# A linear-attention, mixing and MLP kernel: three low parts move to VectorE, a copy and a split move inside the last attention chunk

## The chip, the cores and the metric

The kernel runs on one core of one Trainium2 chip. The metric is the device time of one execution in microseconds (us); less is better. All times inside the execution are counted from the start of the profiled span.

## The reference

Three layers run one after the other on arrays of 4 batches by 768 tokens by 384 channels, all in float32:

```python
# 1. attention, 32 heads of 48 channels, a 48x48 state per head, token by token
y[:, :, t] = einsum('bhd,bhde->bhe', q[:, :, t], state)
v_old = einsum('bhde,bhd->bhe', state, kt)               # kt: normalised key
state = state + bt * einsum('bhd,bhe->bhde', kt, vt - v_old)
# 2. mixing
theta = x @ w_theta
zr, zi = x * cos(theta), x * sin(theta)
u = x + einsum('ts,bsd->btd', w_tok_r, zr) + einsum('ts,bsd->btd', w_tok_i, zi)
x = u + maximum(u @ w_ch, 0)
# 3. layer norm and a two-layer MLP with a residual
xn = (x - mean) / sqrt(var + 1e-6) * g_ln
out = x + maximum(xn @ w_ch1, 0) @ w_ch2
```

## The kernel before

The attention goes through 24 chunks of 32 tokens (`for c in range(1, NC)`). In a chunk two halves h of the heads take turns. For each half TensorE makes `RW[h]` from the state (`R`), VectorE subtracts it from v (`Rs0` or `Rs1`, L440), TensorE multiplies by a triangular inverse (`W_mm`, L452), ScalarE copies the result to `bdw` in four pieces (L458), TensorE updates the state `S` (L466) and ScalarE copies it to `bds` (L471), which the next `R` of that half reads. The outputs of a chunk are summed in `Y[c]` (`py`) by `yq_work` (L481, from the state) and `ym_work` (L492, from `bdw`); `ym_work` ends with a ScalarE copy `ys` (L498) and four stores from SyncE's queue (L501). In the loop `ym_work` of a chunk is issued in the next chunk; that of the last one, 23, stands behind the loop.

In the last chunks the program slips in work of the mixing layer, by `late(c, k)`: k = 0 comes behind the subtraction of half 0, k = 1 behind that of half 1, and k = 2 at the end of the chunk. Every engine takes its instructions in the order in which the program issues them, and an instruction that waits for another engine holds up all behind it on its own engine.

Two things are slipped in. First, weights. They arrive as pairs of 32-bit words (`raw`, two buffers, and one more later) and are made into float32 `t` by five passes on VectorE (in the late steps L777, L787, L788, L797, L798), and then into a high part (ScalarE, L813) and a low part t - high (L820), since TensorE's fp32r keeps fewer bits. One `wts.step()` does the last two passes of one piece, the next step makes its high and low part and the first three passes of the piece behind it, and so on. A piece of the token weights is 128x768; the weights `W[s]` of token tile s are two pieces. The `split` of a piece says how many of its two rows of the low part go to GpSimd; the rest goes to VectorE. It was None (all on GpSimd) for the tiles 0 and 1 and 0 for the others. The load of a piece (L717) is issued on SyncE's queue, when its `raw` buffer is free.

Second, z of the first mixing steps. `mx.theta` multiplies on TensorE, `mx.angles` takes the nearest whole turn on ScalarE (`kk`, L906) and the rest on VectorE (`nf`, L907), `mx.sines` and `mx.cosines` fill `zf` on ScalarE (L914, L915, L922), `mx.turn` multiplies `zf` by x on VectorE (L931) and makes the high part `zh` on ScalarE (L932), and `mx.rest` makes the low part `zl` on VectorE (L938). There is one `zf` buffer: `mx.sines` of a step fills the one that `mx.rest` of the step before it reads.

Behind the attention the mixing steps follow (`mx.mix`, 24 of them, L957 on TensorE), with the weights made by `wts.pump()`, and then the MLP.

Of the kernel before, what the change touches and what calls it, by code (L numbers as in the profile page):

```python
# [16 lines left out]
NC = 24  # L17
# [75 lines left out]
def attention(ctx, tc, kq, ktok, vin, betai, maskin, x, psa, late=None):  # L93
# [32 lines left out]
    def load_kq(c, part=slice(0, 2)):  # L126
        if c < NC:
            if c not in KQ:
                KQ[c] = ring(c).tile([128, 2, 4, 4, 32], F32, name="kqt")
            nc.sync.dma_start(out=KQ[c][:, part], in_=kq[c][:, part])  # L130

    def load_kt(c):
        if c < NC:
            KT[c] = ktp.tile([128, 4, 2, D], F32, name="ktt")
            nc.sync.dma_start(out=KT[c], in_=ktok[c])

    def load_v(c):
        if c < NC:
            V[c] = vp.tile([128, 8, D], F32, name="vt")
            nc.sync.dma_start(out=V[c], in_=vin[c])  # L140

    def scale_v(c):
        if c < NC:
            k = c % 4
            nc.gpsimd.tensor_tensor(out=V[c], in0=V[c], in1=bc(NT[c // 4][:, 8 * k:8 * k + 8].unsqueeze(2), [128, 8, D]),
                                    op=ALU.mult)
# [284 lines left out]
    def R(h, c):  # L431
        if c == 0:
            return V[0][:, 4 * h:4 * h + 4, :]
        b = bds[h][c % 2]
        for g in range(2):
            for r in range(4):
                nc.tensor.matmul(RW[h][32 * r:32 * r + 32, 0, 2 * g:2 * g + 2, :], KQ[c][:, 0, 2 * h + g, r, :],
                                 b[:, 4 * g + r, :, :], start=True, stop=True)
        Rs = p2.tile([128, 4, D], F32, name=f"Rs{h}")
        nc.vector.tensor_tensor(out=Rs, in0=V[c][:, 4 * h:4 * h + 4, :], in1=RW[h][:, 0, :, :], op=ALU.subtract)  # L440
        return Rs

    def W(h, c, Rs):
        W_mm(h, c, Rs)
        W_out(h, c)
# [14 lines left out]
    def S(h, c):  # L460
        b = bdw[h][c % NB]
        if c == NC - 1:
            return
        for g in range(2):
            for e in range(2):
                nc.tensor.matmul(S_ps[h][64 * e:64 * e + D, g, :], KT[c][:, 2 * h + g, e, :],  # L466
                                 b[:, 2 * g + e, :, :], start=(c == 0 and g == 0), stop=True, skip_group_check=True)
        n = bds[h][(c + 1) % 2]
        for e in range(2):
            ee = slice(64 * e, 64 * e + D)  # L470
            nc.scalar.copy(out=n[ee, :, e, :], in_=S_ps[h][ee, :, :].rearrange("p g (r d) -> p (g r) d", r=4))  # L471
# [3 lines left out]
    def yq_work(wk, c):  # L475
        def first():
            Y[c] = psy.tile([128, 2, 4, D], F32, name="py")

        def q(r):
            for g in range(4):  # L480
                nc.tensor.matmul(Y[c][32 * g:32 * g + 32, :, r, :], KQ[c][:, 1, g, r, :],  # L481
                                 bds[g // 2][c % 2][:, 4 * (g % 2) + r, :, :], start=(r == 0), stop=False,
                                 skip_group_check=True)

        wk.add(0.0, first)
        for r in range(4 if c else 0):
            wk.add(0.24, lambda r=r: q(r))

    def ym_work(wk, c):
        def m(e):  # L490
            for g in range(4):
                nc.tensor.matmul(Y[c][32 * g:32 * g + 32, e, :, :], MT[c][:, g, e, :],  # L492
                                 bdw[g // 2][c % NB][:, 2 * (g % 2) + e, :, :], start=(c == 0 and e == 0),
                                 stop=(e == 1),                                 skip_group_check=True)

        def ev():
            ys = p2.tile([128, 2 * 4 * D], F32, name="ys")
            nc.scalar.copy(out=ys, in_=Y[c].rearrange("p e r d -> p (e r d)"))  # L498
            o = 32 * (c % 4)
            for g in range(4):  # L500
                nc.sync.dma_start(out=x[c // 4][o:o + 32, g, :], in_=ys[32 * g:32 * g + 32, :])  # L501

        for e in range(2):
            wk.add(0.4, lambda e=e: m(e))
        wk.add(0.0, ev)
# [27 lines left out]
    def norms():  # L533
        for s in sorted(norm):
            if ("tg", s) in done:
                norm.pop(s)()
        while pend:
            pend.pop(0)()
# [11 lines left out]
    pe = Work()  # L550
# [53 lines left out]
    for c in range(1, NC):  # L604
        s = c // 4
        step[0] = c
        load_kq(c + 11)
        load_v(c + 5)
        scale_v(c + 2)
        load_kt(c + 2)  # L610
        wa, wm, wq = Work(), Work(), Work()
        for n in {1: (9, 10), 2: (11, 12)}.get(c, (c + 10,)):
            if n < NC:
                a_work(wa, n)
        ym_work(wm, c - 1)
        yq_work(wq, c)
        R0 = R(0, c)
        budget = 2.3 if c >= 14 else 3.08
        if c % 4 == 1 and c > 1 and s + 1 < NS:
            while ("tg", s + 1) not in done:  # L620
                dv.step()
        dv.run(budget)
        if late:
            late(c, 0)
        wa.run((0.0 if c == 2 else 0.42) * wa.left())
        S(1, c - 1)
        W(0, c, R0)
        norms()
        wm.flush()
        R1 = R(1, c)  # L630
        dv.run(budget)
        if late:
            late(c, 1)
        if (c % 4 == 3 and s + 1 < NS) or c == 18:
            while s + 1 not in PT:
                if not dv.step():
                    norms()
        wa.flush()
        S(0, c)
        W(1, c, R1)  # L640
        norms()
        wq.flush()
        if c == 13:
            soon.close()
        if c == 18:
            mid.close()
        if c == 19:
            early.close()
        if late:
            late(c, 2)  # L650
    ym_work(pe, NC - 1)
    pe.flush()


def attn_inputs(q, k, v, beta):
# [173 lines left out]
class Mixer:  # L829
# [21 lines left out]
    def load_w(self, s, wtok, pool, wts, w=None):  # L851
        if pool:
            w = [pool.tile([128, 4, C], F32R, name=f"w{s}_{i}") for i in range(2)]
        self.W[s] = w
        for q in range(2):
            r = slice(2 * q, 2 * q + 2)
            wts.add(("w", s, q), wtok[s, q], lambda r=r: self.W[s][0][:, r], lambda r=r: self.W[s][1][:, r],
                    split=0 if s > 1 else None)

    def trans(self, i):  # L860

# [263 lines left out]
def build(tc, a):  # L1125
# [8 lines left out]
    with tc.manual_schedule(), outer:  # L1134
# [11 lines left out]
        mx = Mixer(nc, x, psa, ident, uT)  # L1146
        wts = Weights(nc, None, wide)

        def late(c, k):
            if (c, k) == (13, 2):  # L1150
                xp2 = ph1.enter_context(tc.tile_pool(name="x_", bufs=1, **R))
                x.extend(xp2.tile([128, 4, C], F32, name=f"x{t}") for t in (4, 5))
            if (c, k) == (18, 2):
                nc.gpsimd.memset(ones.bitcast(F32), 1.0)
                nc.scalar.copy(out=ones, in_=ones.bitcast(F32))
                wts.st = ph1.enter_context(tc.tile_pool(name="st", bufs=1, **R))
                mx.load_theta(ph1, tc, a["wth"], wts)
                wts.load()
                nc.sync.dma_start(out=ident, in_=a["ident"])
                nc.sync.dma_start(out=g, in_=a["g"])  # L1160
            if (c, k) == (19, 2):
                mx.open(ph1, tc)
                for s in range(3):
                    mx.load_w(s, a["wtok"], mx.cst if s < 2 else None, wts)
                wts.load()
            if c > 19 or (c, k) == (19, 1):
                wts.step()
            if (c, k) == (16, 2):
                nc.scalar.activation(out=warm, in_=warm, func=AF.Sin)
            if (c, k) == (20, 2):  # L1170
                mx.trans(0)
            if (c, k) == (21, 2):
                mx.theta(0)
                mx.angles(0)
                mx.trans(1)
            if (c, k) == (22, 1):
                mx.sines()
            if (c, k) == (22, 2):
                mx.cosines()
            if (c, k) == (22, 2):  # L1180
                mx.turn(0)
                mx.rest(0)
            if (c, k) == (23, 0):
                mx.theta(1)
                mx.angles(1)
            if (c, k) == (23, 1):
                mx.sines()
            if (c, k) == (23, 2):
                mx.cosines()

        with ExitStack() as att:
            attention(att, tc, a["kq"], a["ktok"], a["vin"], a["betai"], a["mask"], x, psa, late)
# [46 lines left out]
        for i in range(n):  # L1239
            b, s = MIX[i]  # L1240
# [107 lines left out]
```

## Time and profile before

| what | value |
|---|---|
| time, median of 3 runs | 786.51 us (785.75 to 788.28) |
| profiled execution: its time, its span | 786.73 us, 784.8 us |
| mean granted TensorE clock | 0.969 of full speed |
| busy in the span: TensorE, VectorE, ScalarE, GpSimd | 709.4, 517.8, 356.9, 213.2 us |
| TensorE idle before the first mixing matmul of step 2 (at 250.38 us) | 1.89 us |

The profiled execution took 1.93 us more than its span, and 0.22 us more than the median of the runs. The busy times are sums over stages with different limits: the attention ends and the mixing starts near 230 us, and the MLP takes from some 440 us to the end.

### The profile page before, as it was taken

Reading aid. Unit: us, or ns where it says so; the run is one execution under the profiler, and the core shown is the slowest. Engines: PE = TensorE matmul, PEld = TensorE weight load, DVE = VectorE, ACT = ScalarE, POOL = GpSimd, SP = SyncE. Lnnn points to the kernel's source line nnn. Section 1 sums busy time; section 2 is a strip of 40 time slices with the busy share of each in tenths; the row PEclk is TensorE's granted clock in tenths of the full one; section 3 lists DMA queues with packets and bytes.
Section 4 is the critical chain, followed back from the end, with each engine's and each line's share of the span. In section 5 each row is a group of like instructions: output and inputs, shape, how many; then the busy total and the mean of one; then the engine's idle time right before and its main releaser. Section 6 shows DMA issues by size and latency. Waiting matters only on the chain.

```text
span 784.8 us, 18939 instructions
## 1 busy us (share of the span) xinstructions
PE 709.4 (90%) x7955; PEld 655.4 (84%) x7956; DVE 517.8 (66%) x875; ACT 356.9 (45%) x785; POOL 213.2 (27%) x234
## 2 busy tenths in 40 slices
PE   4577887777778999999997999999999999999997
PEld 3455555554468999999997999999999999999997
DVE  7987989986877888888876755435353534444342
ACT  2276776786775766654444433131322222131211
POOL 5854755744020001211111433113131221121120
PEclk8699999999989999999999999999999999999999
DMA  8975767234444223532432220000000000000000
GB/s 250 248 225 172 201 189 214 83 86 137 153 152 162 88 75 101 165 118 80 121 101 81 101 81 5 26 1 31 1 31 1 31 1 30 1 9 24 1 31 30
DMA packets 29716, 71.39 MB, mean 91 GB/s; under 512 B 4928, under 2 KB 17472, under 8 KB 29632
## 3 DMA queue, kind: packets, MB, share of 16 engines
q1 hardware_dynamic: 29632, 70.19, 29.0%
q8 instruction: 62, 1.02, 0.6%
q14 instruction: 22, 0.18, 0.1%
HBM read 56.02 MB, written 9.44 MB: 83 GB/s over the span
## 4 chain that ended last, share of the span: by engine, by line
PE 64%; DVE 15%; DMA 6%; ACT 6%; issue 5%; POOL 2%; SPq 1%; ACTq 0%; DVEq 0%; POOLq 0%
PE ph L1071 19%; PE acc L1090 19%; PE y L957 11%; PE pc L1012 5%; PE pth L897 3%; DMA bdk<-kq 3%; DVE prod L369 2%; ACT bdw L458 2%; DMA raw<-wtok 2%; PE py L492 1%; PE S L466 1%; PE pa L174 1%; DVE t L797 1%; PE RW L452 1%; DVE Ti L378 1%
## 5 line engine op out<-in xcount | busy, mean ns | idle before, releaser
L957 PE MATMUL y<-w,zh 128*128 128x384 f32 x576 | 154.8, 342 | 3.4 <-DVE u L966 2.4
L1090 PE MATMUL acc<-hh,f 128*128 128x384 f32 x576 | 147.0, 336 | 0.0
L1076 DVE SCALAR_TENSOR_TENSOR hl<-ph,hh 128x384 fp32r<-128x384 f32 x96 | 52.4, 553 | 114.5 <-ACT hh L1075 114.5
L1075 ACT ACTIVATE hh<-ph 128x384 fp32r<-128x384 f32 x96 | 46.7, 491 | 163.0 <-PE ph L1071 163.0
L1071 PE MATMUL ph<-xh,f 128*128 128x384 f32 x576 | 116.4, 337 | 0.4 <-DVE u L966 0.4
L957 PEld LDWEIGHTS y<-w,zh 128*128 128x128 f32 x576 | 105.8, 190 | 4.2 <-issue 2.7
L1090 PEld LDWEIGHTS acc<-hh,f 128*128 128x128 f32 x576 | 104.5, 188 | 0.0
L1071 PEld LDWEIGHTS ph<-xh,f 128*128 128x128 f32 x576 | 101.9, 188 | 0.7 <-issue 0.7
L957 PE MATMUL y<-w,zl 128*128 128x384 f32 x288 | 97.7, 339 | 2.4 <-DVE zl L938 2.4
L1090 PE MATMUL acc<-hl,f 128*128 128x384 f32 x288 | 96.9, 336 | 0.0
L1071 PE MATMUL ph<-xl,f 128*128 128x384 f32 x288 | 65.7, 336 | 0.0
L458 ACT COPY bdw<-RW 32x192 f32<-32x192 f32 x192 | 59.5, 310 | 13.6 <-PE RW L452 11.0
L957 PEld LDWEIGHTS y<-w,zl 128*128 128x128 f32 x288 | 54.6, 190 | 3.0 <-DVE zl L938 3.0
L471 ACT COPY bds<-S 48x384 f32<-48x384 f32 x92 | 43.5, 472 | 29.0 <-PE S L466 27.4
L466 PE MATMUL S<-bdw,ktt 128*48 128x192 f32 x368 | 42.0, 351 | 14.4 <-ACT bdw L458 14.3
L1090 PEld LDWEIGHTS acc<-hl,f 128*128 128x128 f32 x288 | 54.0, 188 | 0.0
L806 POOL TENSOR_TENSOR t<-t,g 128x384 f32<-128x384 f32 x12 | 15.3, 1279 | 135.3 <-DVE t L798 123.3
L1071 PEld LDWEIGHTS ph<-xl,f 128*128 128x128 f32 x288 | 51.6, 188 | 0.0
L452 PEld LDWEIGHTS RW<-Rs,pt 32*32 32x32 f32 x1472 | 19.8, 109 | 36.6 <-DVE Rs L440 28.5
L452 PE MATMUL RW<-Rs,pt 32*32 32x48 f32 x1472 | 26.4, 210 | 21.4 <-DVE Rs L440 21.0
L466 PEld LDWEIGHTS S<-bdw,ktt 128*48 128x48 f32 x368 | 20.8, 128 | 28.7 <-ACT bdw L458 22.2
L1100 POOL TENSOR_TENSOR o<-u,o 128x384 f32<-128x384 f32 x21 | 20.8, 1017 | 85.0 <-DVE o L1099 85.0
(165 smaller groups left out, 1305.8 us busy)
## 6 DMA issues: line engine op xcount, KB each, us to landing
kqt<-kq SPq DMA_DIRECT2D x20, 512.0 KB, 5.5
raw<-wtok SPq DMA_DIRECT2D x12, 768.0 KB, 4.7
raw<-wff SPq DMA_DIRECT2D x12, 768.0 KB, 4.9
bdk<-kq SPq DMA_DIRECT2D x40, 192.0 KB, 4.0
vt<-vin SPq DMA_DIRECT2D x24, 192.0 KB, 4.9
ktt<-ktok SPq DMA_DIRECT2D x24, 192.0 KB, 4.6
x<-ys SPq DMA_DIRECT2D x96, 48.0 KB, 2.5
flat<-t SPq DMA_DIRECT2D x12, 384.0 KB, 5.5
```

Of the source, the lines that this page charges most:

```text
L452: nc.tensor.matmul(RW[h][rr, 1, j, :], PT[c // 4][rr, m0 + j, :], Rs[rr, j, :], start=True, stop=True)
L458: nc.scalar.copy(out=b[rr, :, r, :], in_=RW[h][rr, 1, :, :])
L466: nc.tensor.matmul(S_ps[h][64 * e:64 * e + D, g, :], KT[c][:, 2 * h + g, e, :], b[:, 2 * g + e, :, :], start=(c == 0 and g == 0), stop=Tru ...
L471: nc.scalar.copy(out=n[ee, :, e, :], in_=S_ps[h][ee, :, :].rearrange("p g (r d) -> p (g r) d", r=4))
L897: nc.tensor.matmul(ps, l[:, k], self.tw[w][:, k], start=(n == 0), stop=(n == 8))
L957: nc.tensor.matmul(self.Y[q], l[:, ri, 128 * k:128 * k + 128], self.W[s][w][:, 2 * ri + h], start=(first and w == ri == 0 and l is zh), st ...
L1012: nc.tensor.matmul(ps, self.wc[w][:, k, 128 * e:128 * e + 128], r[:, k], start=(n == 0), stop=(n == 8))
L1071: nc.tensor.matmul(ps, w[:, 0, 128 * k:128 * k + 128], r[:, k], start=(n == 0), stop=(n == 8))
L1075: nc.scalar.activation(out=hh, in_=ps, func=AF.Relu)
L1076: nc.vector.scalar_tensor_tensor(out=hl, in0=ps, scalar=0.0, in1=hh.bitcast(F32), op0=ALU.max, op1=ALU.subtract)
L1090: nc.tensor.matmul(self.ACC[j][e], w[:, 1, 128 * e:128 * e + 128], r, start=(f == 0 and n == 0), stop=(f == NF - 1 and n == 2))
L1100: (nc.vector if j == NJ - 1 else nc.gpsimd).tensor_tensor(out=o, in0=u[:, e], in1=o, op=ALU.subtract)
```

## The change

Three things are changed. The low parts of the pieces of tiles 0 and 1 (four pieces) are made by VectorE. `mx.turn(0)` moves from the end of chunk 22 to the first late step of chunk 23, in front of `mx.theta(1)`, and `mx.rest(0)` to its second late step. `ym_work` of chunk 23 is issued at the end of the loop's last turn, in front of `late(23, 2)`, which holds the last weight step of the attention and `mx.cosines`.

```diff
@@ attention, end of the chunk loop
         if c == 19:
             early.close()
+        if c == NC - 1:
+            ym_work(pe, c)
+            pe.flush()
         if late:
             late(c, 2)
-    ym_work(pe, NC - 1)
-    pe.flush()
@@ Mixer.load_w
             wts.add(("w", s, q), wtok[s, q], lambda r=r: self.W[s][0][:, r], lambda r=r: self.W[s][1][:, r],
-                    split=0 if s > 1 else None)
+                    split=0)
@@ build, late(c, k)
             if (c, k) == (22, 2):
                 mx.cosines()
-            if (c, k) == (22, 2):
+            if (c, k) == (23, 0):
                 mx.turn(0)
-                mx.rest(0)
-            if (c, k) == (23, 0):
                 mx.theta(1)
                 mx.angles(1)
             if (c, k) == (23, 1):
+                mx.rest(0)
                 mx.sines()
```

The lines behind L648 stand one lower in the changed kernel (L813 is its L814, L820 its L821, L932 its L933).

On VectorE, from the last pass over the piece `t_3990` (first half of tile 1) to the first passes over `t_4062` (second half of tile 1; `t_4057` after), this is the order before. `Rs0` and `Rs1` are the subtractions of chunk 23:

```order
L798 SCALAR_TENSOR_TENSOR t_3990<-raw_3901,t_3990 128x768
L931 TENSOR_TENSOR zf_3996<-zf_3996,x0_69 128x768
L938 TENSOR_TENSOR zl_4046<-zf_3996,zh_4045 128x768
L440 TENSOR_TENSOR Rs0_4058<-vt_3379,RW0_126 128x192
L777 TENSOR_SCALAR t_4062<-raw_3994 128x768
L787 TENSOR_SCALAR t_4062<-t_4062 128x768
L788 TENSOR_SCALAR t_4062<-t_4062 128x768
L907 SCALAR_TENSOR_TENSOR nf_4079<-kk_4078,pth_4068 128x384
L440 TENSOR_TENSOR Rs1_4130<-vt_3379,RW1_127 128x192
```

And this is the order of the changed kernel, from the same pass to the low part behind `zl`:

```order
L799 SCALAR_TENSOR_TENSOR t_3990<-raw_3901,t_3990 128x768
L440 TENSOR_TENSOR Rs0_4053<-vt_3379,RW0_126 128x192
L821 TENSOR_TENSOR w1_1_3651<-t_3990,w1_0_3650 128x768
L778 TENSOR_SCALAR t_4057<-raw_3994 128x768
L788 TENSOR_SCALAR t_4057<-t_4057 128x768
L789 TENSOR_SCALAR t_4057<-t_4057 128x768
L932 TENSOR_TENSOR zf_3996<-zf_3996,x0_69 128x768
L908 SCALAR_TENSOR_TENSOR nf_4078<-kk_4077,pth_4067 128x384
L440 TENSOR_TENSOR Rs1_4129<-vt_3379,RW1_127 128x192
L798 SCALAR_TENSOR_TENSOR t_4057<-raw_3994,t_4057 128x768
L799 SCALAR_TENSOR_TENSOR t_4057<-raw_3994,t_4057 128x768
L939 TENSOR_TENSOR zl_4064<-zf_3996,zh_4063 128x768
```

`zf` of step 0 now stands behind the three passes over the newly loaded piece, and `zl` behind its last two; the low part of `w1` is new.

On ScalarE, from the high part of z of step 0 to the copy of chunk 23's outputs (`ys_4191`), this is the order before:

```order
L932 CAST zh_4045<-zf_3996 128x768
L813 CAST w1_0_3650<-t_3990 128x768
L906 ACTIVATE kk_4078<-pth_4068,magic_3517 128x384
L471 COPY bds1_1_117<-S1_125 48x8x48 x2
L458 COPY bdw0_2_120<-RW0_126 32x4x48 x4
L498 COPY ys_4116<-py_4025 128x384
L914 ACTIVATE zf_4134<-nf_4079 128x384
L915 ACTIVATE kk_4078<-nf_4079 128x384
L458 COPY bdw1_2_123<-RW1_127 32x4x48 x4
L813 CAST w1_0_3650<-t_4062 128x768
L922 ACTIVATE zf_4134<-kk_4078,halfpi_3515 128x384
L498 COPY ys_4191<-py_4157 128x384
```

The same stretch in the changed kernel, where `ys_4182` is that copy:

```order
L814 CAST w1_0_3650<-t_3990 128x768
L933 CAST zh_4063<-zf_3996 128x768
L907 ACTIVATE kk_4077<-pth_4067,magic_3517 128x384
L471 COPY bds1_1_117<-S1_125 48x8x48 x2
L458 COPY bdw0_2_120<-RW0_126 32x4x48 x4
L498 COPY ys_4115<-py_4025 128x384
L915 ACTIVATE zf_4134<-nf_4078 128x384
L916 ACTIVATE kk_4077<-nf_4078 128x384
L458 COPY bdw1_2_123<-RW1_127 32x4x48 x4
L498 COPY ys_4182<-py_4157 128x384
L814 CAST w1_0_3650<-t_4057 128x768
L923 ACTIVATE zf_4134<-kk_4077,halfpi_3515 128x384
```

`zh` of step 0 and the high part of `w1` have changed places, with the chunk's `kk`, `bds1` and `bdw0` behind them as before; `ys` of chunk 23 now stands in front of the last high part of `w1`.

## Rows read from the trace of the kernel before

**Rows 1.** The chain that ended last: start us, us, what.

```profile
218.48 5.18 DMA raw<-wtok
...
228.65 1.45 PE py L492 x16
...
235.72 0.97 DVE t L798
...
236.71 4.17 DMA raw<-wtok
...
250.38 4.78 PE y L957 x17
```

**Rows 2.** Windows: stretch, us; busy (x count) by engine; PEclk, DMA share, GB/s.

```profile
228.00:230.00 2.00, 2.00 (x34) 1.43 (x24) 1.75 (x4) 1.89 (x4) 0.51 (x1) 0.50 0.50 130
253.00:255.00 2.00, 2.00 (x9) 2.00 (x7) 1.93 (x4) 1.51 (x3) 0.00 (x0) 0.57 0.00 0
290.00:330.00 40.00, 40.00 (x236) 39.86 (x235) 34.24 (x49) 24.01 (x43) 6.48 (x5) 1.00 0.40 129
```

**Rows 3.** Timeline of VectorE: start us, us, what [idle before it <- releaser].

```profile
208.78 2.18 DVE L788 TENSOR_SCALAR t<-t 128x768 uint32<-128x768 uint32 x1
...
215.39 0.56 DVE L788 TENSOR_SCALAR t<-t 128x768 uint32<-128x768 uint32 x1
215.98 2.55 DVE L797 SCALAR_TENSOR_TENSOR t<-raw,t 128x768 uint32<-128x768 uint32 x1
218.56 0.96 DVE L798 SCALAR_TENSOR_TENSOR t<-raw,t 128x768 uint32<-128x768 uint32 x1
...
221.30 0.96 DVE L938 TENSOR_TENSOR zl<-zf,zh 128x768 fp32r<-128x768 f32 x1 [0.90 <-ACT zh L932]
222.18 0.34 DVE L440 TENSOR_TENSOR Rs<-vt,RW 128x192 f32<-128x192 f32 x1
223.76 0.62 DVE L777 TENSOR_SCALAR t<-raw 128x768 uint32<-128x768 uint32 x1 [1.24 <-DMA raw<-wtok]
...
225.95 0.35 DVE L440 TENSOR_TENSOR Rs<-vt,RW 128x192 f32<-128x192 f32 x1
...
231.48 0.56 DVE L883 TENSOR_TENSOR xl<-pt,xh 128x384 fp32r<-128x384 f32 x1 [1.67 <-ACT xh L879]
...
239.65 0.95 DVE L820 TENSOR_TENSOR w<-t,w 128x768 fp32r<-128x768 f32 x1
```

**Rows 4.** Timeline of ScalarE.

```profile
207.78 0.84 ACT L813 CAST w<-t 128x768 fp32r<-128x768 f32 x1
...
214.95 0.84 ACT L813 CAST w<-t 128x768 fp32r<-128x768 f32 x1
...
220.44 0.83 ACT L932 CAST zh<-zf 128x768 fp32r<-128x768 f32 x1 [1.03 <-DVE zf L931]
...
222.03 0.58 ACT L906 ACTIVATE kk<-pth,magic 128x384 f32<-128x384 f32 x1
222.51 0.94 ACT L471 COPY bds<-S 48x384 f32<-48x384 f32 x2
...
226.06 0.52 ACT L914 ACTIVATE zf<-nf 128x384 f32<-128x384 f32 x1 [0.81 <-DVE nf L907]
...
227.28 1.27 ACT L458 COPY bdw<-RW 32x192 f32<-32x192 f32 x4 [0.28 <-PE RW L452]
...
230.15 0.48 ACT L498 COPY ys<-py 128x384 f32<-128x384 f32 x1 [0.22 <-PE py L492]
```

**Rows 5.** Timeline of GpSimd.

```profile
208.69 1.84 POOL L820 TENSOR_TENSOR w<-t,w 128x768 fp32r<-128x768 f32 x1 [20.09 <-ACT w L813]
215.86 1.85 POOL L820 TENSOR_TENSOR w<-t,w 128x768 fp32r<-128x768 f32 x1 [5.33 <-ACT w L813]
```

**Rows 6.** Timeline of SyncE's queue.

```profile
215.08 3.31 SPq L501 DMA_DIRECT2D x<-ys  x4
```

**Rows 7.** Timeline of TensorE.

```profile
223.73 0.60 PE L437 MATMUL RW<-bds,kqt 128*32 128x96 f32 x16
```

## The prediction

> **What bounds the kernel now.** I read the chain of work that ended last first, then the windows, then each engine's timeline from 205 to 260 us, since the change touches nothing else. From 290 to 330 us TensorE is busy in all of 40 us at full clock [rows 2], and from 250.38 us on the chain runs through its mixing matmuls [rows 1]. All that comes behind is issued in an order that does not change, on engines that wait for each other step by step, so what moves the start at 250.38 moves the end by as much. In front of it the chain goes back to a weight load at 236.71 us, which begins 0.02 us after the last pass over an earlier piece, the L798 that starts at 235.72 and ends at 236.69 [rows 1]: the load waits for that buffer. From there to 250.38 the instructions are the same in both kernels. **The end of that L798 is my checkpoint**: what it loses, the kernel loses. Ahead of it stand VectorE's passes, another load (issued at 218.48, landed after 5.18 us), `Rs1` of chunk 23 at 225.95, TensorE's products for the last output, ending at 230.10, and the split of x for step 2, L883 at 231.48 [rows 1, 3].
>
> **Low parts on VectorE, up to `Rs0` of chunk 23.** Two of the four low parts on GpSimd stretch a pass on VectorE beside them: L788 takes 2.18 us beside the one at 208.69, L797 2.55 beside the one at 215.86 [rows 3, 5]. The other L788 takes 0.56, and two-input passes of that size 0.95 [rows 3]. So 1.62 + 1.60 us come back. The price is four low parts of 0.95 us on VectorE (0.88 to the next start, as from `zl` at 221.30 to `Rs0` at 222.18) [rows 3], each behind ScalarE's high part. The first high part ends at 207.78 + 0.84 = 208.62 [rows 4]. VectorE would have gone on at 207.59 (two passes, 0.59 apart, ahead of the L788 at 208.78); now it does at 208.65 + 0.88 = 209.53, 1.94 late, and less 1.62 that is +0.32. The second high part, as much later, ends at 214.95 + 0.84 + 0.32 = 216.11 [rows 4], and the passes that began at 214.20 (0.59 each ahead of those at 215.39 and 215.98) begin at 217.02: +2.82, less 1.60, so their last one, L798, ends at 220.74 instead of 219.52 [rows 3]. The edit loses 1.2 us there. `Rs0`, however, no longer stands behind `zf` and `zl`: it starts at 220.65 instead of 222.18 [rows 3], 1.5 us early.
>
> **z of step 0 in chunk 23, up to `Rs1`.** The third low part waits for its high part (220.77 to 221.61) and leaves VectorE free at 222.5. The next pass needs the load that landed at 223.66 [rows 1]. Its issue stands behind four stores, which took 3.31 us from 215.08 [rows 6]; 0.3 later, that is 218.8. Before, the next load followed as soon as the L798 ended at 219.52; now it waits for 220.74, so the first flies more alone, and its time lies between the rows 4.17 and 5.18 [rows 1], near the shorter. I take L777 at s = 222.9. Bounds: 222.5 (VectorE is not free before) and 224.0 (5.18 again).
>
> `zf` follows three passes later, at s + 1.72 (before, `nf` stood there, with `Rs1` 0.47 behind it at s + 2.19 [rows 3]), and ends at s + 2.68. ScalarE's `zh` waits for it, as it did for 1.03 us before [rows 4]; but now `kk` and the `bds1` copies of chunk 23 are queued behind it. `zh` 0.83 (0.74 to the next start), `kk` 0.48 (222.03 to 222.51), `bds1` 0.94 [rows 4]: done at s + 4.9. TensorE's R of half 1 takes 0.60 [rows 7], or some 0.9 if the idle time has lowered its clock, and `Rs1` starts at s + 5.7 = 228.6 instead of 225.95: **+2.65** (bounds 228.0 and 229.85, so +2.05 and +3.9). The early `Rs0` is of no use, since R waits for `bds1`.
>
> **From `Rs1` (its start is r) to x's split.** This took 5.53 us, from 225.95 to 231.48 [rows 3]. Now the sine of step 1 writes the one `zf` buffer that `zl` of step 0 still reads, and `zl` stands behind `Rs1` and two passes: 0.27 + 0.99 + 0.88 + 0.96, ending at r + 3.1. Queued behind the sine on ScalarE are its twin L915 and the last four `bdw1` copies. Sine and twin take 0.85 (0.52 [rows 4], overlapping), the copies 1.27 [rows 4]: r + 5.3. The last product needs these copies for six of its eight parts, 6/8 of 1.45 = 1.1 [rows 1], and ends at r + 6.4, where it was r + 4.15. Then ScalarE copies `ys` (0.48 [rows 4], 0.4 to the next start) and, by the third edit, only now makes the last high part, 0.84: r + 7.65. VectorE's fourth low part waits for that (0.88), and behind it come the three passes over the fifth piece, which lay under TensorE's products before (0.59 + 0.59 + 0.48). L883 starts at r + 10.2: **+4.7**, give or take 0.2 for the gaps. About 2.3 of it is the wait of the sine, 2.4 the low part and the passes that lost their cover.
>
> From L883 to the checkpoint's L798 the order is the same: 0. The weight load that SyncE now issues behind the last eight stores is needed by VectorE just behind the checkpoint, at r + 15.4. With 3.31 us for four stores [rows 6] from r + 6.9 and 4.17 to land [rows 1] it is there at r + 14.5, and ScalarE's pass over it ends just in time: 0 too.
>
> **Sum:** 2.65 + 4.7 = 7.35 us, bounds 6.55 and 8.8. On the profiled execution, 786.73 + 7.35 = 794.1; that execution stood 0.22 above the median of the runs, so 793.8 or 793.9 beside it.
>
> **The clock.** TensorE's granted clock was 0.50 from 228 to 230 us, behind waits in chunk 23, and 0.57 from 253 to 255, behind its wait for step 2 [rows 2]: the lower level, 1.2 GHz, for most of these stretches. Two us at 0.57 lose 2 x 0.43 = 0.86 us, here on the path. The change makes the idle times longer (some 5 us in chunk 23, some 3 in front of step 2's start), so such a stretch can move under the wait and vanish (-0.9) or last 4 us longer (+1.7). I take 0 and keep both ends.
> The Trainium skill (TensorE: Matmul & The Clock Gate, section "Why this matters for your kernels") advises against idle gaps between bursts of matmuls, because the clock drops behind them. By that rule the last rival below is what happens; that a low clock follows a wait agrees with the 0.50 and 0.57 of [rows 2].
>
> **The rivals.**
> - *Faster.* The early `Rs0` carries on to the end and the waits for ScalarE find cover: 1.5 us gained, 785.0. It decides if `zf` is ready when ScalarE comes to `zh` at 221.6, for which the load must have landed 2.68 us before, at 218.9. Against it: the load cannot be issued before the copy `ys` ends at about 215.4, and with no time at all for the four stores 4.17 us more make 219.6. Chance 0.05.
> - *No change.* The lateness goes into waits that TensorE has anyway. Its wait at 250.38 is this same chain's, and the load at 236.71 starts 0.02 us after what it waits for [rows 1], so there is no slack to fill. Chance 0.04.
> - *One wait only.* If the sine does not wait for `zl`, the `bdw1` copies end at r + 2.6 (R's product 0.4 + 0.9 behind `Rs1`, then 1.27), the last product at r + 4.15 as before, the high part at r + 5.4, L883 at r + 8.0: +2.5 instead of +4.7, 791.6. There is one buffer; chance 0.10.
> - *The clock stays low* in the first mixing steps: 1.7 us or more on top, 795.6 to 798. Chance 0.13.
>
> **How the numbers follow.** The forecast, both waits, has 0.68: 792.4 to 796 by its own bounds with little from the clock. The range of 8 in 10 goes from the one-wait case with 0.9 us of clock gained, 790.5, to the middle of the low-clock case, 797.0. About 0.3% (2.4 us) is what a measurement of this kernel can tell from no change. Slower by more than that are the forecast, one wait and low clock, 0.91 together; faster 0.05; the same 0.04.
>
> **What would show it.** In the changed profile: no GpSimd work between 190 and 270 us and no VectorE pass stretched there; `Rs0` of chunk 23 near 220.6 and `Rs1` near 228.6; `zh` of step 0 waiting some 4 us for `zf`, with `kk` and `bds` right behind it; the sine of step 1 waiting for `zl`; the last high part of `w1` behind `ys`, and VectorE idle some 4 us for it; x's split near 238.8 and the checkpoint's end near 244. The prediction is wrong if `Rs1` comes before 227, if step 2 does not start some 7 us later than 250.38, or if it does and the end does not follow.

## The result, and the profile after

| | before | after |
|---|---|---|
| time, median of 7 runs (lowest to highest) | 785.75 us (783.61 to 788.46) | 791.70 us (790.29 to 793.20) |
| ratio of the times, 95% interval | | 1.0075 (1.0053 to 1.0096) |
| profiled execution: its time, its span | 786.73, 784.8 us | 791.70, 789.8 us |
| busy: TensorE, VectorE, ScalarE, GpSimd | 709.4, 517.8, 356.9, 213.2 us | 710.5, 517.3, 355.9, 205.8 us |

The changed kernel is slower by 0.75%, some 5.9 us. The busy times hardly move; GpSimd is spared 7.4 us, the four low parts that it made before (the title says three; four move), and nothing comes of it. The loss is in waits of the last attention chunk. Here is the chain that ended last in the changed kernel (start us, us, what), from the load for the fourth weight piece to the load behind the checkpoint.

```profile
217.11 4.50 DMA raw<-wtok
221.63 0.57 DVE t L778
222.22 0.57 DVE t L788
222.82 0.56 DVE t L789
223.38 0.88 DVE zf L932
224.34 0.83 ACT zh L933
225.19 0.58 ACT kk L907
226.14 0.48 ACT bds L471
226.67 0.91 PE RW L437 x16
...
229.82 0.88 DVE zl L939
231.21 0.51 ACT kk L916
...
232.94 0.87 PE py L492 x12
234.31 0.74 ACT w L814
235.07 0.96 DVE w L821
...
242.82 4.01 DMA raw<-wtok
```

It is the chain of the prediction, step for step: load, three passes, `zf`, `zh`, `kk`, `bds1`, R, then `zl`, the sine's twin, the last product, the last high part, its low part. In [rows 1] `py` ended 11.62 us behind the issue of the load (218.48 to 230.10); here it ends 16.70 us behind it (217.11 to 233.81). VectorE's timeline of the changed kernel (start us, us, instruction, idle before it and what ended it) shows where it stood still:

```profile
204.49 0.96 DVE L799 SCALAR_TENSOR_TENSOR t<-raw,t 128x768 uint32<-128x768 uint32 x1
206.66 0.96 DVE L821 TENSOR_TENSOR w<-t,w 128x768 fp32r<-128x768 f32 x1 [1.22 <-ACT w L814]
...
214.15 0.96 DVE L821 TENSOR_TENSOR w<-t,w 128x768 fp32r<-128x768 f32 x1 [1.54 <-ACT w L814]
...
218.67 0.35 DVE L440 TENSOR_TENSOR Rs<-vt,RW 128x192 f32<-128x192 f32 x1
219.65 0.96 DVE L821 TENSOR_TENSOR w<-t,w 128x768 fp32r<-128x768 f32 x1 [0.63 <-ACT w L814]
221.63 0.56 DVE L778 TENSOR_SCALAR t<-raw 128x768 uint32<-128x768 uint32 x1 [1.02 <-DMA raw<-wtok]
...
227.60 0.35 DVE L440 TENSOR_TENSOR Rs<-vt,RW 128x192 f32<-128x192 f32 x1 [1.24 <-PE RW L437]
...
235.07 0.96 DVE L821 TENSOR_TENSOR w<-t,w 128x768 fp32r<-128x768 f32 x1 [4.38 <-ACT w L814]
...
237.60 0.55 DVE L884 TENSOR_TENSOR xl<-pt,xh 128x384 fp32r<-128x384 f32 x1
...
241.84 0.96 DVE L799 SCALAR_TENSOR_TENSOR t<-raw,t 128x768 uint32<-128x768 uint32 x1
```

The first row is the last pass over the first piece of tile 0. It is issued ahead of every difference between the kernels, so I count from its start, the **anchor**: 206.72 us before, 204.49 after. The last row is the checkpoint's pass. No pass is stretched to 2.18 or 2.55 us any more [rows 3], but each low part waits for ScalarE, the last one for 4.38 us. ScalarE in turn waits for VectorE, twice:

```profile
224.34 0.83 ACT L933 CAST zh<-zf 128x768 fp32r<-128x768 f32 x1 [4.72 <-DVE zf L932]
...
230.78 0.52 ACT L915 ACTIVATE zf<-nf 128x384 f32<-128x384 f32 x1 [2.36 <-DVE zl L939]
...
231.62 1.26 ACT L458 COPY bdw<-RW 32x192 f32<-32x192 f32 x4
...
233.83 0.48 ACT L498 COPY ys<-py 128x384 f32<-128x384 f32 x1 [0.94 <-PE py L492]
234.20 0.83 ACT L814 CAST w<-t 128x768 fp32r<-128x768 f32 x1
```

The waits before `zh` and the sine were 1.03 and 0.81 us [rows 4]. TensorE meanwhile has nothing to do:

```profile
226.67 0.87 PE L437 MATMUL RW<-bds,kqt 128*32 128x96 f32 x16 [6.27 <-ACT bds L471]
```

The first wait therefore reaches TensorE as 6.27 us. R then took 0.87 us, 0.60 before [rows 7], at the lower clock level, as the windows of the changed kernel show (PEclk is the third figure from the end). In a second trace of the kernel before (b2_before, below) R took 0.87 us as well, so these 0.27 us need not be the change's.

```profile
226.00:228.00 2.00, 0.87 (x16) 0.52 (x16) 0.76 (x3) 1.91 (x7) 0.00 (x0) 0.50 0.00 0
...
236.00:238.00 2.00, 2.00 (x8) 2.00 (x8) 1.93 (x5) 0.00 (x0) 0.00 (x0) 0.53 0.34 80
...
256.00:258.00 2.00, 1.71 (x10) 1.71 (x11) 1.17 (x3) 1.23 (x3) 0.00 (x0) 1.00 0.77 307
```

The second window lies in the first mixing step, at the lower level again; the chain above does not run through TensorE there. The third holds the start of mixing step 2 (its first product with `zl`), at 256.29 us, and its clock is full; before, 253 to 255 us had 0.57 [rows 2].

Split at these places, the span's +5.0 us are four terms:

| stretch | before | after | difference |
|---|---|---|---|
| start to anchor | 206.72 | 204.49 | -2.23 |
| anchor to the checkpoint's end ("the stretch") | 29.96 | 38.31 | +8.35 |
| checkpoint's end to the start of step 2 | 13.70 | 13.49 | -0.21 |
| start of step 2 to the end ("the tail") | 534.42 | 533.51 | -0.91 |

The change acts in the second row. Among the traces below, the anchor lies anywhere from 202.71 to 209.16 us, and two executions of one and the same kernel (x_zhsine and x_zhsine2) have it at 203.83 and 207.33, so the first row is a difference between executions.

### The profile page after: what moved, and what is told of

Read it like the earlier page. It is cut to its first block, busy times and chain, and to the rows that moved or that the text cites. A ratio compares the mean times of both kernels' runs of the same rounds, so it can differ in the third digit from the quotient of the medians.

```text
span 789.8 us, 18937 instructions
## 1 busy us (share of the span) xinstructions
PE 710.5 (90%) x7956; PEld 655.7 (83%) x7956; DVE 517.3 (66%) x879; ACT 355.9 (45%) x785; POOL 205.8 (26%) x230
## 3 DMA queue, kind: packets, MB, share of 16 engines
q8 instruction: 62, 1.02, 0.5%
## 4 chain that ended last, share of the span: by engine, by line
PE 57%; DVE 21%; ACT 8%; issue 5%; DMA 4%; POOL 3%; SPq 1%; ACTq 0%; DVEq 0%; POOLq 0%
PE ph L1072 19%; PE acc L1091 19%; PE y L958 6%; PE pc L1013 5%; DVE prod L369 3%; ACT bdw L458 3%; DVE zl L939 2%; DMA raw<-wtok 2%; PE pth L898 2%; DVE XT L378 2%; DVE t L799 2%; DVE t L798 2%; DVE zf L932 1%; PE S L466 1%; DMA bdk<-kq 1%
## 5 line engine op out<-in xcount | busy, mean ns | idle before, releaser
L958 PE MATMUL y<-w,zl 128*128 128x384 f32 x288 | 99.3, 345 | 2.4 <-DVE zl L939 2.2
```

The source lines that it names most:

```text
L958: nc.tensor.matmul(self.Y[q], l[:, ri, 128 * k:128 * k + 128], self.W[s][w][:, 2 * ri + h], start=(first and w == ri == 0 and l is zh), st ...
```

## The experiments

The theory: two waits of ScalarE (`zh` for `zf`; the sine for `zl`) hold up the state copies, `bdw1` and the last product, and the third edit takes away the cover of the last low part. Rivals: the low parts themselves are what is slow; the third edit is; one of the two waits alone is. "Stretch" is read from one trace of each kernel, the ratio from its timed runs against runs of before of the same set; the two traces of before give 29.96 and 30.35.

| kernel | stretch, us | ratio to before (95%) |
|---|---|---|
| after | 38.31 | 1.0075 (1.0053 to 1.0096) |
| x1_low: edit 1 alone | 31.10 | 0.9998 (0.9979 to 1.0017) |
| x2_turn: edit 2 alone | 36.47 | 1.0063 (1.0038 to 1.0088) |
| x3_copy: edit 3 alone | 31.46 | 1.0013 (0.9993 to 1.0033) |
| x13: edits 1 and 3 | 32.35 | 1.0022 (1.0004 to 1.0040) |
| x_sine: after, sine moved back | 35.90 | 1.0066 (1.0042 to 1.0091) |
| x_zh: after, `zh` moved back | 34.82 | 1.0061 (1.0039 to 1.0084) |
| x_zhsine: after, both moved | 33.54 | 1.0006 (0.9988 to 1.0024) |
| x_zhsine2: the same once more | 32.52 | 1.0042 (1.0023 to 1.0061) |
| x12_zhsine: the same without edit 3 | 31.27 | 0.9991 (0.9972 to 1.0009) |
| g_defer: edit 1, low parts deferred | 30.13 | 0.9988 (0.9969 to 1.0007) |
| g_both: g_defer, stores from GpSimd | 29.77 | 0.9971 (0.9953 to 0.9988) |

**Edit 1 alone** (x1_low):

```diff
-                    split=0 if s > 1 else None)
+                    split=0)
```

> The first edit alone: the four low parts of tiles 0 and 1 on VectorE, the rest as before. The stretch that I compare runs from the start of the last pass over the first piece of tile 0 to the issue of the load behind the checkpoint: 29.99 us before, 38.33 in the changed kernel (+8.34). My theory (the waits on ScalarE's queue and the lost cover make the loss, not VectorE's longer work): +1.3 us in the stretch, time 0.1 to 0.2% over before. Rival (VectorE's added 3.8 us of low parts are what the kernel lost): +4 us or more, 0.5%.

**Edit 2 alone** (x2_turn):

```diff
             if (c, k) == (22, 2):
                 mx.cosines()
-            if (c, k) == (22, 2):
-                mx.turn(0)
-                mx.rest(0)
             if (c, k) == (23, 0):
+                mx.turn(0)
                 mx.theta(1)
                 mx.angles(1)
             if (c, k) == (23, 1):
+                mx.rest(0)
                 mx.sines()
```

> The second edit alone: z of step 0 begun in chunk 23, low parts on GpSimd, the last copy as before. My theory: ScalarE's high part of z waits for VectorE with the chunk's copies behind it, and the sine of step 1 waits for the low part of z with the last copies behind it: +5.8 us in the stretch (3.5 up to the second subtraction of chunk 23, 2.3 behind it), up to 6.5 if GpSimd's low part stretches a pass; 0.6 to 0.8% over before. Rival (the edits only cost together): under +2 us.

**Edit 3 alone** (x3_copy):

```diff
             early.close()
+        if c == NC - 1:
+            ym_work(pe, c)
+            pe.flush()
         if late:
             late(c, 2)
-    ym_work(pe, NC - 1)
-    pe.flush()
```

> The third edit alone: the last output copy in front of the last weight step. My theory: ScalarE makes the last high part 1.9 us later and x's split about 1 us later, behind the copy that waits for TensorE: +1.0 to +1.6 us in the stretch, 0.1 to 0.2% over before. Rival (the copy's earlier place frees PSUM and stores sooner): 0 or a gain.

Against the first trace of before, edit 1 alone lengthens the stretch by 1.1 us, edit 3 by 1.5, edit 2 by 6.5 of the whole change's 8.35; the timed runs put the same edit first. The time of x1_low, expected at 0.1 to 0.2% over before, doesn't show it: the interval reaches from 0.9979 to 1.0017. That edit 2 needs neither of the others for its two waits is seen on ScalarE in x2_turn:

```profile
228.96 0.83 ACT L932 CAST zh<-zf 128x768 fp32r<-128x768 f32 x1 [6.01 <-DVE zf L931]
...
235.40 0.52 ACT L914 ACTIVATE zf<-nf 128x384 f32<-128x384 f32 x1 [2.36 <-DVE zl L938]
```

The wait for `zl` is 2.36 us, as after. That the low parts on VectorE are the slow part falls with x1_low. The last one waits there for only 0.97 us, against 4.38 after (VectorE of x1_low):

```profile
226.09 0.96 DVE L820 TENSOR_TENSOR w<-t,w 128x768 fp32r<-128x768 f32 x1 [0.97 <-ACT w L813]
```

In x3_copy the last high part stands ahead of `xh` on ScalarE, and x's split waits longer for `xh` (2.47 us on VectorE, 1.67 before [rows 3]):

```profile
232.97 0.56 DVE L884 TENSOR_TENSOR xl<-pt,xh 128x384 fp32r<-128x384 f32 x1 [2.47 <-ACT xh L880]
233.45 1.36 DVE L932 TENSOR_TENSOR zf<-zf,x 128x768 f32<-128x768 f32 x1
```

The second row is a further 0.4 us of its 1.5: this pass took 0.95 us before, and now lies beside GpSimd's last low part, which begins at 232.13 and takes 1.86 us.

**Edits 1 and 3** (x13, the diffs of x1_low and x3_copy together):

> The first and third edit, without the second. My theory: +0.8 us up to the second subtraction of chunk 23, then +2.5, as the last high part behind the copy now holds up the low part and three passes on VectorE: +3.2 us in the stretch, 0.3 to 0.4% over before, and so 5 us less than with all three edits. Rival (the low parts on VectorE carry the loss whatever z does): near the +8.3 of all three.

The stretch grows by 2.4 us, less than forecast and about the sum of the two alone (2.6): without edit 2 the two do not make each other dearer. The time, 1.0022, is 1.7 us.

**The sine moved back** (x_sine, against the changed kernel):

```diff
             if (c, k) == (23, 1):
                 mx.rest(0)
-                mx.sines()
             if (c, k) == (23, 2):
+                mx.sines()
                 mx.cosines()
```

> The changed kernel with the sine of step 1 and its twin moved behind the last high part (to the last late step), so that the last four copies of the attention no longer stand behind an instruction that waits for the low part of z. My theory: the stretch is 2.2 us shorter than in the changed kernel (36.1 of 38.33), the time 0.3% below it, 0.5% over before. Rival (the last product waits for something else, the sine's wait was only listed there): no change against the changed kernel.

**`zh` moved back** (x_zh): `turn` leaves out the copy for step 0, and it is issued in the second late step.

```diff
             if (c, k) == (23, 0):
-                mx.turn(0)
+                mx.turn(0, True)
                 mx.theta(1)
...
             if (c, k) == (23, 1):
+                nc.scalar.copy(out=mx.Z[0][0], in_=mx.ZF2)
                 mx.rest(0)
```

> The changed kernel with ScalarE's high part of z of step 0 moved behind the copies of half 0 of chunk 23 (to its second late step); VectorE's product stays in its place. My theory: the second subtraction of chunk 23 comes 2.6 to 3 us earlier and the rest is as in the changed kernel: the stretch is 35.5 of 38.33, time 0.35% below the changed kernel. Rival (the second subtraction waits for VectorE's passes anyway): no change.

Each takes one wait out, and only the one. In x_sine ScalarE still waits for `zf`, but the `bdw1` copies are free of the sine:

```profile
222.94 0.83 ACT L933 CAST zh<-zf 128x768 fp32r<-128x768 f32 x1 [4.48 <-DVE zf L932]
...
227.54 1.27 ACT L458 COPY bdw<-RW 32x192 f32<-32x192 f32 x4 [0.53 <-PE RW L452]
```

In x_zh the state copies go ahead of `zh`, and the sine still waits:

```profile
218.70 0.94 ACT L471 COPY bds<-S 48x384 f32<-48x384 f32 x2
...
222.46 0.83 ACT L1187 CAST zh<-zf 128x768 fp32r<-128x768 f32 x1 [1.01 <-DVE zf L932]
...
225.92 0.52 ACT L915 ACTIVATE zf<-nf 128x384 f32<-128x384 f32 x1 [2.63 <-DVE zl L940]
```

The stretch falls by 2.4 and by 3.5 us. The times do not follow: both kernels stay at 0.6%, where 0.3% and 0.35% less than the changed kernel were expected. Taken from 1.0075, the fall of the stretch would give 1.0044, which the interval of x_sine still holds, and 1.0031, which that of x_zh does not. Their profiled executions, 788.47 and 787.17 us, lie well under their medians (791.41 and 791.71), in part because they reach the anchor early (203.33 and 203.12 us). How much of a single move is real in time stays open.

**Both moved** (x_zhsine, the two diffs together), and **the same without edit 3** (x12_zhsine):

> Both moves together: neither the copies of half 0 nor those of half 1 stand behind a wait for VectorE. My theory: what is left is the third edit's cost on top of the low part, +2.5 to +3.5 us against before in the stretch (32.5 to 33.5), 0.3 to 0.4% over before. Rival (the low parts on VectorE are the loss): near the 38.3 of the changed kernel.

> As the last one, and with the third edit undone: the low parts on VectorE and z of step 0 in chunk 23, but with no wait on ScalarE ahead of the chunk's copies and the last output copy behind the loop again. My theory: +0.5 us against before in the stretch (30.5), time within 0.15% of before. Rival (VectorE's added work): 33 us or more.

The first gave a stretch 3.2 to 3.6 us over before, but a time only 0.06% over it. I ran it again unchanged:

> The changed kernel with both ScalarE moves once more, unchanged from the run of that name, since its time (0.06% above before, interval -0.12 to +0.24%) and its one traced execution (stretch 33.54 us, 3.2 to 3.6 above the two traces of before) disagree. If the traced stretch is typical and the timed runs were lucky: stretch again 33 to 34 us, and a ratio of 1.002 to 1.004. If the traced execution was the untypical one (a late landing of one weight load in it): a stretch of 30.5 to 32 us, and again a ratio of 0.999 to 1.002. If both repeat (33 to 34 us and no more than 1.001), something behind or ahead of the stretch gives the lost time back in the runs, and neither reading of the chain is complete.

Neither reading held cleanly. The second trace has 32.52 us, between the two forecasts, and the second ratio is 1.0042. The two intervals, from 0.9988 to 1.0024 and from 1.0023 to 1.0061, hardly touch, though the kernel is one and the same: the interval of one set of runs doesn't cover what differs between two sets. In the traces the landing of a load is most of the difference: the first pass over the landed piece starts 17.36 us from the anchor in the first and 16.66 in the second, and these 0.70 us stand in `Rs1` as well; the stretches differ by 1.02. The middle of the two ratios, 1.0024, is 1.9 us, against 2.2 to 3.6 us of stretch. With both waits out, most of the loss is gone, in the stretch and in this middle; by the second ratio alone it is less than half. In x_zhsine2 the last low part still waits 2.05 us; without edit 3, in x12_zhsine, 0.41 (VectorE of each):

```profile
232.12 0.96 DVE L821 TENSOR_TENSOR w<-t,w 128x768 fp32r<-128x768 f32 x1 [2.05 <-ACT w L814]
```

```profile
231.13 0.96 DVE L820 TENSOR_TENSOR w<-t,w 128x768 fp32r<-128x768 f32 x1 [0.41 <-ACT w L813]
```

That is the cover which edit 3 takes away. x12_zhsine, with the low parts on VectorE and step 0's z in chunk 23, can't be told from before in time (0.9991); its stretch is 0.9 to 1.3 us longer, 0.5 was expected.

**Before again** (b2_before, one execution, no edit), to see how far one trace can be trusted:

> The kernel before, once more, for a second trace: the changed kernel's profile reached the last pass over the first piece of tile 0 at 204.49 us where before it was 206.72, though nothing ahead of that place differs. If that is chance between executions, this trace lies elsewhere than 206.72 by a us or two, and the stretch to the load is again 30.0 us within 0.4. If it belongs to the change, it is again 206.7.

It took 785.58 us; its anchor is at 206.23, its stretch 30.35 and its tail 533.27 us. So 0.4 us of a stretch and 1.2 us of a tail are chance. The anchor moved by only 0.49 us, which decides nothing; that it moves by execution is shown by x_zhsine and x_zhsine2.

**Low parts deferred** (g_defer): edit 1 alone, but VectorE makes each low part one weight step later, when its high part is long ready. The diff is cut: `step` begins by making the low parts put off.

```diff
-        lows = [self.parts(*u) for u in self.two]
+        lows, self.lows = self.lows + [self.parts(*u) for u in self.two], []
...
-            self.parts(*u)()
+            f = self.parts(*u)
+            if u[0][5] is None:
+                self.lows.append(f)
+            else:
+                f()
```

> The kernel before with the first edit and each of these low parts put off to the next weight step, where ScalarE's high part is long done; nothing else. My theory (the price of the low parts was the wait for ScalarE): the stretch is 0.7 to 1.3 us shorter than before (28.7 to 29.3), time 0.1% under before. Rival (VectorE's added work costs what it takes): 2 to 3 us longer.

**Stores from GpSimd's queue as well** (g_both): the stores of `ys` no longer stand ahead of the weight loads on SyncE's queue.

```diff
-                nc.sync.dma_start(out=x[c // 4][o:o + 32, g, :], in_=ys[32 * g:32 * g + 32, :])
+                (nc.gpsimd if c >= 20 else nc.sync).dma_start(out=x[c // 4][o:o + 32, g, :], in_=ys[32 * g:32 * g + 32, :])
```

> As the last one, and with the output stores of chunks 20 to 23 issued from GpSimd's queue, so that the weight load that VectorE waits for in chunk 23 is not behind them on SyncE's queue. My theory: that load lands some 4 us earlier, the second subtraction of chunk 23 comes 2 us earlier, the stretch is 2 us shorter than before (28.0), time 0.25% under before. Rival (GpSimd's issues are held up beside VectorE's passes and the stores come late): no gain over the last one.

Both missed in the stretch: 30.13 and 29.77 us, where before has 29.96 and 30.35. The 1.6 us that the first stretched pass gives back go into the next wait. VectorE in g_defer:

```profile
209.58 0.56 DVE L795 TENSOR_SCALAR t<-t 128x768 uint32<-128x768 uint32 x1
211.54 0.55 DVE L914 SCALAR_TENSOR_TENSOR nf<-kk,pth 128x384 f32<-128x384 f32 x1 [1.40 <-ACT kk L913]
```

This is the pass that took 2.18 us before; now it takes 0.56, and `nf` behind it waits 1.40 us for ScalarE's `kk`. The stretch had lain over a wait. The second trace of before shows the same without an edit. There the pass starts at 208.29 us, just ahead of GpSimd's low part (208.52), and is not stretched; `nf` waits 1.78 us and starts 4.40 us from the anchor, no earlier than in the first trace (4.16). VectorE of b2_before:

```profile
208.29 0.56 DVE L788 TENSOR_SCALAR t<-t 128x768 uint32<-128x768 uint32 x1
210.63 0.55 DVE L907 SCALAR_TENSOR_TENSOR nf<-kk,pth 128x384 f32<-128x384 f32 x1 [1.78 <-ACT kk L906]
```

In g_defer two low parts of 0.88 us come on top, so the second and the third piece are done 1.2 and 0.4 us later from the anchor than before (8.53 and 13.18 us, against 7.29 and 12.80). In g_both the load comes in time, as forecast: its first pass starts right behind `Rs0`. But `Rs1` starts 19.18 us from the anchor (19.23 and 19.77 in the two traces of before), as it now waits 0.94 us for R, which stands behind two products on TensorE at a granted clock of 0.56 (224.4 to 228.0 us). g_both is 0.29% faster than before, by an interval that excludes 1, and the only version clearly ahead of before. Why is not shown: its stretch is 0.2 to 0.6 us shorter at best, its traced execution (788.08 us) was the slowest of its 12, and x_zhsine shows a ratio moving by 0.36% between two sets of runs. I don't count it as a proven gain.

## Why the prediction was right, step by step

Direction, place and mechanism came out as forecast: 793.8 us predicted, 791.7 measured. That the totals are so near is partly luck, as the sum at the end shows. The prediction's own sign, step 2 some 7 us later than 250.38, reads 5.91 us from the start of the span (256.29) and 8.14 us from the anchor. Counted from the anchor (before / forecast / after), by the prediction's steps:

- **Up to `Rs0`.** The last pass over the third piece ends at 12.80 / 14.02 / 14.26 us, `Rs0` starts at 15.46 / 13.93 / 14.18. The loss of 1.2 measured 1.46 us, the early `Rs0` 1.3 us instead of 1.5. As said, the early `Rs0` was of no use. What the prediction didn't see is that 1.4 us or more of the first stretched pass lay over the wait for `kk` (g_defer, b2_before); it subtracted 1.62 for that pass and the error, 0.24 us, is small because the wait for the high part covered `kk` in the changed kernel.
- **Up to `Rs1`: the term that was mis-sized**, +2.65 forecast, +3.88 measured (19.23 to 23.11; +3.34 against b2_before), inside its bounds of +2.05 and +3.9. The queue on ScalarE was nearly right: from the first pass over the landed piece to `Rs1` 5.97 us, 5.7 forecast, 2.19 before. What failed is "I take L777 at s = 222.9", a pass starting 0.86 us earlier than before; it started 0.10 later, at 17.14 us against 17.04. The flight was shorter than before, but less so than forecast (4.50 us; 5.18 before [rows 1], 4.1 in the forecast), and the load was issued 0.86 later, where 0.3 was taken: the four stores ahead of it began 0.56 later, because the passes behind VectorE's first low part did, and held the queue 0.3 longer. SyncE's queue after (start, us, x count):

```profile
213.41 3.60 SPq L501 DMA_DIRECT2D x<-ys  x4
217.11 2.00 SPq L718 DMA_DIRECT2D raw<-wtok  x2
```

- **From `Rs1` to x's split.** +4.7 forecast, +4.47 measured (5.53 to 10.00 us). Behind `Rs1`, `zl` ended after 3.1 us (3.1 forecast), the `bdw1` copies after 5.3 (5.3), the last product after 6.2 (6.4), the high part after 7.4 (7.65). x_sine and x_zhsine2 bear out the split of this term: without the sine's wait it is 7.83 and 7.66 us.
- **From x's split to the checkpoint.** 0 forecast, 5.20 us in both kernels. From the start of step 2 to the end the two differ by 0.91 us, the clock's part.
- **The clock.** The forecast took 0 between -0.9 and +1.7; the trace has -0.91 in the tail, where the stretch at 0.57 is gone. That this is a merit of the change is not shown: b2_before has no such stretch either. Of the 14 traces only before, g_defer and g_both have it. The rival of a low clock in the first mixing steps came true in part (0.53 from 236 to 238 us) and cost nothing, as x's split and the checkpoint are on VectorE and ScalarE. The Trainium skill (TensorE: Matmul & The Clock Gate, "Why this matters for your kernels"), which the prediction cited, advises against idle gaps between bursts of matmuls, because the clock drops behind them. That agrees with the attention, where R ran at 0.50 behind the idle 6.27 us, though R of b2_before took 0.87 us with no more than 1.96 us of idle close ahead of it; and it did not decide anything behind step 2's start.
- **The sum.** +7.35 forecast for the stretch, +8.35 traced (+7.96 against b2_before). In time it was +5.9 us. In the traced pair the anchor took back 2.2 and the tail 0.9, both of which I hold for chance; but most of the other timed excesses, too, lie below what the stretch alone would give (x2_turn 5.0 of 6.5 us, x1_low none of 1.1). The traces show nothing behind the checkpoint that gives time back, but the clock: from its end to the end of the span 546.8 to 547.3 us pass in eleven of them, the changed kernel and b2_before among them, and 547.9 to 548.1 in the three with the low clock behind step 2's start. If most runs of before have that low clock, about 1 us of the difference is explained. Whether they do is open, and so is the rest.

"One wait only" (791.6 us) is nearest to the measured time, and wrong all the same: both waits are in the trace. A right total says little about which terms made it.

## What to carry to other kernels

An operation in an engine's in-order queue costs what is behind it: `zh`, 0.83 us long, held up two state copies that TensorE needed and turned into 6.27 us of idle. So before moving work to an earlier slot, ask when its input is ready, and put copies that feed the critical engine ahead of it. Judge a stretched pass by what follows it: if the instruction behind it waits for another engine anyway, removing the stretch returns nothing.

## What was not expected of the hardware

- The same matmuls, behind the same wait of 1.89 us, are granted the lower clock in one execution and full clock in another. These are the windows near step 2's start in b2_before, which stay at 1.00, and in g_both, at 0.53, beside 0.57 in [rows 2]:

```profile
253.00:255.00 2.00, 2.00 (x14) 1.97 (x13) 1.93 (x4) 1.56 (x3) 0.00 (x0) 1.00 0.00 0
```

```profile
252.00:254.00 2.00, 1.98 (x6) 1.98 (x7) 0.89 (x2) 1.51 (x3) 0.00 (x0) 0.53 0.81 332
```

  The tails are 533.27 and 534.28 us: the low stretch costs about 1 us on the path, and it comes by execution.
- The attention's instructions up to the anchor are the same in all these kernels but g_both, and the anchor is reached at 202.71 us in one execution (x1_low) and at 209.16 in another (x2_turn); for one and the same kernel it was 203.83 and 207.33 (x_zhsine, x_zhsine2). That spread of 6.5 us is larger than the change itself, so two single traces are compared from a common anchor, not from the start of the span.
